# Joined small-tile stretches, one bfloat16 run per pair of the down projection, and a new order of small transfers in SP's queue

## The chip, the cores and the metric

The kernel runs on one core of one Trainium2 chip. The metric is the device time of one execution in microseconds. Engines are named as in the profile: PE (TensorE), PEld (its weight loads), DVE (VectorE), ACT (ScalarE), POOL (GpSimd) and SP (SyncE, which here only issues transfers; "SPq" is its queue). All but one of the transfers are issued by SP, in the order in which its instructions stand.

## What is computed

One transformer block with adaptive layer normalisation, S = 2048 rows of D = 1024, 32 heads of width 32, F = 3584, all in bfloat16:

```
sa, ca, ga, sb, cb, gb = silu(c) @ w_mod          # six rows of 1024
h   = layernorm(x) * (1 + ca) + sa
q, k, v = h @ wqkv ; pq, pk = phi(q), phi(k)      # phi(t) = t+1 if t>0 else exp(t), + 1e-6
kv  = pk^T v ; z = sum_s pk                       # per head
o   = (pq kv) / (pq z + 1e-6)
x   = x + ga * (o @ wo)
h   = layernorm(x) * (1 + cb) + sb
x   = x + gb * ((gelu(h @ w_gate) * (h @ w_up)) @ w_down)
```

## The kernel before, in words

A small recording layer (`sch.op`, `sch.dma`) notes every operation with what it reads and writes, derives the semaphore waits, and emits one instruction stream per engine, in the order recorded. Between two marks (from the end of the first k products to the second unit of the feed-forward part) `reorder` sorts the streams of DVE, ACT and POOL by a table of costs and due times; PE and SP keep the written order everywhere. SP's transfers run on eight semaphore lanes in turn, so a transfer also waits until the one eight places ahead of it has landed.

The stages on PE, with their places in the profiled execution:

- **q and k** (to about 127 us): layer norm, `q_block` and `kv_mm` products.
- **M** (127 to 191 us): instead of v, the kernel forms M = pk^T x, group by group (`m_tile`, L895: 16 matmuls of 128 x 341 or 342 make one tile; 24 tiles; output in PSUM banks 0 to 3 in turn). ACT copies each tile to MB, SP transposes MB by a transfer (`m_t`, notes mT0 to mT7, into two MTB buffers), and `kv_prod` (L913, eight 128 x 128 matmuls) multiplies by the v weights. The dictionary `HOOK` hangs other work behind tile n: "kv3" is `kv_prod(3)`; "modp" is `mod_pass` (eight matmuls on 32-column tiles, a copy, a store, and the loads sbT and cbT of the second shift and scale); "z32" prepares the denominators' weights; "den0" and "den1" are `den` (32 matmuls on 32-column tiles, then 1/den on DVE, L1245 and L1246, and a store to memory, the notes rden0.st and rden1.st); "w1" is `w2_pair(1)` (eight matmuls on 64 x 64 tiles); "gbr" is `gb_rows` (eight on 32-column tiles); "ps" is `pq_scale`, "rb" is `rb_load`: four transfers of 256 KB each that read 1/den back, broadcast over partitions, into RB. `rb_load(2, ...)` and `rb_load(1)` wait for rden1.st.
- **wo** (191 to about 257 us): after the last tile PE does parts of `wo_mm` (L1283), `w2_pair(2)`, `kv_prod(6)`, `kv_prod(7)`, `w2_pair(3)`, and then the chunks c0 to c15 of the output projection, two PSUM banks each, 2(c mod 4) and the next. DVE multiplies PQ by RB (`pq_scale`, L1273: four pieces per half of 512 rows, noted pqs sg.h.g0), adds each chunk to x (x1, L1291), and applies scale and shift of the second layer norm (h2mod, L724, which needs cb1, L1767, made from cbT). ACT makes the normalised rows, SP transposes them by transfers (T2). The dictionary `SLOT` hangs work behind chunk c; slot 2 held the scaling of PQ 1 and the load x7 of rows 7 to 9, slot 4 held cb1 and the first feed-forward weights (`wt_dma(0)`, two transfers).
- **feed-forward** (241 to 598 us): 28 units, each of seven products P1 to P7 (a Strassen-like scheme with sums ss and tp in fp32r; unit 0 runs P1, P2, P5, P6 before the rest of wo). P5 and P6 of unit 0 read ssum0 and ssum1 (L1413).
- **down projection** (598 us to the end): eight pairs of row chunks. In each pair `d_pair` runs seven products of 14 matmuls each in the order 1, 5, 6, 2, 7, 3, 4: P1 and P2 are bfloat16, the others fp32r. Their left sides are sums S0 to S4 (`d_s`, L1648; two halves each, S4 copied by ACT) of the activations ya.0 and ya.1, loaded by `y_in`; ACT copies (`dpcp`, `descp`) and DVE adds (`dpadd`, L1695) combine the banks b0 to b0+3; `evac` (L1576, L1577) scales, adds x and stores; `x_in` loads x (xq).

The matmul stream of M and the head of the wo stage stand in the code as

```
        for n, (g, k) in enumerate(tiles):
            m_tile(g, k, n % 4, n % 2)
            if n == len(tiles) - 1:
                kv_prod(5, 4)
            if k == 2:
                m_t(g)
            ...
            for f in HOOK.get(n, "").split():
                hook_run(f)
```

Of the kernel before, what the change touches and what calls it, by code (L numbers as in the profile page):

```python
# [8 lines left out]
ALU = mybir.AluOpType  # L9
# [321 lines left out]
def bass_adaLN_cond__linear_attn_block__geglu_ffn__prompt_kernel(  # L331
# [18 lines left out]
    with ExitStack() as es:  # L350
# [554 lines left out]
        def m_t(g):  # L905
            i = g % 2
            tdma(Q, MTB[i][:, :, :], MB[g][:, :], r_mb(g), r_mtb(i), f"mT{g}")

        def kv_prod(g, bank):
            i = g % 2  # L910
            o = None
            for dc in range(NDC):
                o = sch.op(T, lambda e, dc=dc: e.matmul(PS(bank, 0, P), WV[:, g, dc, :], MTB[i][:, dc, :],  # L913
                                                        start=(dc == 0), stop=(dc == NDC - 1)),
                           rd=r_wv(g) + r_mtb(i), pwr=(pr(bank) if dc == 0 else ()), note=f"kv g{g} dc{dc}")
            pset_writer(bank, o)
            z = 64 * (g % 2)
            for h in range(2):
                a, gz = 64 * h, g // 2 * 2 + h
                sch.op(V, lambda e, a=a, gz=gz: e.tensor_tensor(KVT[z:z + 64, gz, 0:64], ps_all[a:a + 64, bank * 512 + a:bank * 512 + a + 64], BMASK[a:a + 64, a:a + 64], ALU.mult),  # L920
                       prd=pr(bank), rd=r_sm("bmask"), wr=r_kvt(gz, gz + 1), note=f"kvt{g}", overwrite_ok=True)
# [270 lines left out]
        def z32():  # L1192
            sch.op(V, lambda e: e.tensor_tensor(Z32[:], BM32[:], ZCOLS[:, :].unsqueeze(2).to_broadcast([P, NG, NH]), ALU.mult),
                   rd=r_sm("bm32") + r_sm("zcols"), wr=r_sm("z32"), note="z32")

        def w2_pair(i, b0=4):
            for hf in range(2):
                for r in range(2):
                    for h in range(2):
                        b, g = b0 + 2 * r + hf, 2 * i + h  # L1200
                        sch.op(T, lambda e, b=b, g=g, h=h, r=r, hf=hf: e.matmul(ps_all[64 * h:64 * h + 64, b * 512:(b + 1) * 512], KVT[64 * r:64 * r + 64, g, 0:64],  # L1201
                               WO[64 * r:64 * r + 64, g, hf * 512:(hf + 1) * 512], start=True, stop=True),
                               rd=r_kvt(g, g + 1) + r_wo(g, hf * 512, (hf + 1) * 512), pwr=pr(b), note=f"w2 {i}.{hf}", overwrite_ok=True)
            for r in range(2):
                b, g = b0 + 2 * r, 2 * i + r
                w_, p_ = W2[:, g, :], ps_all[:, b * 512:(b + 2) * 512]
                eng = V if i > 1 and r else A
                sch.op(eng, lambda e, w_=w_, p_=p_, eng=eng: e.activation(w_, p_, ACTF.Copy) if eng == A else e.tensor_copy(w_, p_),
                       prd=pr(b) + pr(b + 1), wr=r_w(OFF_WK, "w2", g), note=f"w2cp{g}")
# [15 lines left out]
        def mod_pass():  # L1225
            assert mdone[0] >= 48 and not late
            mod_rows(((2, 4, 5, hl_src),))
            o_r = mod_store(4, 5, MROW[1], r_2k(OFF_ROW + 2048, "mrow1"), 1)
            for dst, nt, a0 in ((SBT, "sbT", 0), (CBT, "cbT", 2)):
                sch.dma(Q, lambda e, dst=dst, a0=a0: e.dma_start(dst[:, :], scr_row[1, a0:a0 + 2, :].rearrange("a (b p) -> p (a b)", p=P)),  # L1230
                        wr=r_sm(nt), deps=[o_r], note=nt)

# [33 lines left out]
        GH = [((0, 2), (2, 4)), ((4, 6), (6, 8))]  # L1266

        def pq_scale(sg, h, gs):
            i, t0 = sg % 2, h * HW
            for g0, g1 in gs:  # L1270
                ap = PQ[sg][:, g0:g1, t0:t0 + HW]
                rng = r_pq(sg, g0, g1, t0, t0 + HW)
                sch.op(V, lambda e, ap=ap, i=i, h=h, g0=g0, g1=g1: e.tensor_tensor(ap, ap, RB[i][:, h, g0:g1, :], ALU.mult),  # L1273
                       rd=rng + r_rb(i, h, g0, g1), wr=rng, deps=rb_ops[sg, h], note=f"pqs{sg}.{h}.{g0}")

        x1_ops, s_ops = {}, {}

        def wo_mm(c_, b0, gs):
# [9 lines left out]
            if gs[-1] == NG - 1:  # L1288
                for half in range(2):
# [3 lines left out]
                       prd=pr(b0) + pr(b0 + 1), rd=r_x(c_), wr=r_x(c_) + r_smc("st", c_, 48),  # L1293
                       deps=[s_ops[0, 0, 1]] if c_ == 13 else [], note=f"x1 c{c_}")
                if c_ < 2 * CPG:
# [5 lines left out]
        tiles = [(g, k) for g in range(4) for k in range(3)] + [(g, 0) for g in range(4, NG)] + [(g, k) for g in range(4, NG) for k in (1, 2)]  # L1301
        HOOK = {0: "ga", 6: "kv0", 10: "kv1", 11: "w0", 13: "kv2", 15: "modp kv3 z32", 16: "den0", 17: "w1 rb0.0 rb0.1", 18: "",
                19: "kv4", 20: "den1 ps0.0", 21: "gbr", 22: "ps0.1", 23: "rb2.0"}
        st = {}

        def hook_run(f):
# [11 lines left out]
            elif f[:3] == "den":  # L1318
                st[int(f[3:])] = den(int(f[3:]), 5)
                st[int(f[3:])]()  # L1320
# [7 lines left out]
        for n, (g, k) in enumerate(tiles):  # L1328
# [39 lines left out]
        def wt_dma(u):  # L1368
            i, f0 = u % 2, u % NFP * 256
            for t, v_ in enumerate((wg_v, wu_v)):  # L1370
                sch.dma(Q, lambda e, t=t, v_=v_: e.dma_start(WT[i][:, t, :, :], v_[:, :, f0:f0 + 256]), wr=r_wt(i, t, t + 1), note=f"wt{t} u{u}")

# [282 lines left out]
        def d_prod(ca, b0, k, own=None, js=None):  # L1655
            b = b0 + {1: 0, 2: 0, 5: 3, 6: 2, 7: 2, 4: 2, 3: 1}[k] if own is None else own
            i = {1: None, 2: None, 5: 0, 6: 1, 7: 2, 3: 3, 4: 4}[k]
            o = None
            js = range(nj(ca)) if js is None else js
            for j in js:  # L1660
# [5 lines left out]
                else:  # L1666
# [3 lines left out]
                    if i == 4:  # L1670
                        dst = dst.rearrange("p (h c) -> p h c", h=2)
                o = sch.op(T, lambda e, l_=l_, r_=r_, j=j, dst=dst: e.matmul(dst, l_[:, 0, :], r_, start=(k in (1, 5) or own is not None) and j == js[0], stop=j == js[-1], skip_group_check=True),  # L1672
                           rd=rl + rr, pwr=(pr(b) if j == js[0] else ()), note=f"down P{k} c{ca} j{j}", overwrite_ok=True)
# [30 lines left out]
        def d_pair0(hook):  # L1704
            parts = parts_of(0)
            for k in (2, 6, 5, 0, 7, 3, 13, 11, 12, 4):
# [13 lines left out]
                hook(k)  # L1720

        def d_pair(i, hook):
            ca, b0 = 2 * i, i % 2 * 4
# [6 lines left out]

            for k in (1, 5, 6, 2, 7, 3, 4):
                if last and k == 3:
                    d_prod(ca, b0, 3, None, range(6, NDJ))
                    evac_part(*parts[1])
                    continue
                d_prod(ca, b0, k)
                if k == 1:
                    d_cp(b0 + 2, b0, "dpcp")
                elif k == 5:
                    d_ecp(b0 + 3)  # L1740
                    d_s(ca, 2)
                elif k == 6:
                    d_add(b0 + 1, b0 + 2)
                    d_s(ca, 3)
                    y_next(0)
                elif k == 2:
                    evac(*parts[0])
                elif k == 7:
                    d_add(b0 + 3, b0 + 2)
                    d_s(ca, 4)  # L1750
                    y_next(1)
                    evac(*parts[3])
                elif k == 3:
# [12 lines left out]
        def cb1():  # L1766
            sch.op(V, lambda e: e.tensor_scalar(CB1T[:, :], CBT[:, :], 1.0, None, op0=ALU.add), rd=r_sm("cbT"), wr=r_sm("cb1T"))  # L1767
# [116 lines left out]
        def hooks(i):  # L1884
            def hook(k):
                more = i + 1 < 2 * CPG
                if i == 1:
                    if k == 1:
                        d_t(2, 5)
                        d_t(2, 6)  # L1890
                    if k in (6, 2, 7):
                        d_t(4, {6: 4, 2: 5, 7: 6}[k])
                    if k in (6, 7):
                        n = 1 if k == 6 else 2
                        evac(*parts_of(0)[n])
                        x_in(1, n)
                else:
                    if k == 1:
                        x_in(i, 0, 3, 1)
                    elif k == 5:  # L1900
                        x_in(i, 2)
                    if not more and k in (5, 6):
                        for q in {5: (0, 1), 6: (2,)}[k]:
                            t_gb(q)
            return hook

        d_pair0(hook0)
        for i in range(1, 2 * CPG):
            d_pair(i, hooks(i))
# [75 lines left out]
```

## Time and profile before

| what | value |
|---|---|
| time, median of 3 runs | 782.52 us (782.25 to 782.95) |
| span of the profiled execution (its own time between first and last instruction) | 780.9 us |
| median minus that span | 1.6 us |
| granted TensorE clock, mean | 1.000 |
| PE busy | 770.2 us (99%) |
| DVE busy | 645.9 us (83%) |
| ACT busy | 374.6 us (48%) |
| share of the chain that ended last on PE | 95% |

Starts are microseconds from the start of the span. A line of the timeline gives start, length (first start to last end of a merged group), engine, line of the kernel, operation, out<-in, and the number of instructions. A matmul line shows a pipelined length; the distance between starts is what a matmul costs. Some matmul records are missing, weight loads (PEld) are complete.

### The profile page before, as it was taken

How to read it: one execution, taken by the hardware profiler on the slowest of the kernel's cores; microseconds unless marked ns; L12 is line 12 of the kernel's file. 1: busy time of each engine (PE TensorE's matmuls, PEld its weight loads, DVE VectorE, ACT ScalarE, POOL GpSimd, SP SyncE). 2: the span in 40 equal slices, each digit the busy share in tenths (PEclk: the TensorE clock that was granted, in tenths of full speed). 3: DMA queues.
4: the chain of work that ended last, by engine and by line, in shares of the span. 5: the costliest groups of instructions: out<-in, count | busy, mean ns of one | idle time of the engine just before them, and what ended most of it. 6: DMA issues, size and time to landing. Idle time of an engine off the chain costs nothing.

```text
span 780.9 us, 10753 instructions
## 1 busy us (share of the span) xinstructions
PE 770.2 (99%) x3825; PEld 496.2 (64%) x3883; DVE 645.9 (83%) x964; ACT 374.6 (48%) x629; POOL 47.5 (6%) x126
## 2 busy tenths in 40 slices
PE   8999999999999999999999999999999999999998
PEld 4444445666445667667676767667676576677766
DVE  6699988897899878787989888888989888676767
ACT  2497743242466487878755555555555211111111
POOL 2031300000321011100000000000000000000000
PEclk9999999999999999999999999999999999999999
DMA  9879749939999358867353865535356334443331
GB/s 284 256 167 252 158 91 215 255 80 196 203 287 231 82 138 212 230 175 215 99 145 108 250 211 172 148 96 161 97 147 221 111 127 139 144 141 114 126 125 60
DMA packets 196940, 130.22 MB, mean 167 GB/s; under 512 B 69516, under 2 KB 182420, under 8 KB 195864
## 3 DMA queue, kind: packets, MB, share of 16 engines
q1 hardware_dynamic: 196872, 129.55, 62.4%
q8 instruction: 30, 0.49, 0.3%
q14 instruction: 22, 0.18, 0.1%
q10 hardware_dynamic: 16, 0.00, 0.0%
HBM read 92.55 MB, written 23.35 MB: 148 GB/s over the span
## 4 chain that ended last, share of the span: by engine, by line
PE 95%; SPq 2%; DMA 1%; DVE 1%; issue 1%; ACT 0%; DVEq 0%; ACTq 0%
PE ps_all L1458 45%; PE ps_all L1672 21%; PE ps_all L895 7%; PE ps_all L934 7%; PE ps_all L1283 7%; PE ps_all L880 5%; PE ps_all L1593 1%; SPq L598 1%; DMA wmq<-in_w_mod_dram 1%; SPq L603 1%; DMA h1T<-xh 0%; PE ps_all L913 0%; PE ps_all L1201 0%; PE ps_all L1240 0%; DVE h1T L724 0%
## 5 line engine op out<-in xcount | busy, mean ns | idle before, releaser
L1458 PE MATMUL ps_all<-ss,tp 128*128 128x512 f32 x896 | 214.3, 396 | 0.0
L1458 PEld LDWEIGHTS ps_all<-ss,tp 128*128 128x128 f32 x896 | 168.3, 188 | 37.8 <-DVE ss L1413 0.2
L1672 PE MATMUL ps_all<-dt,sb 128*128 128x512 f32 x424 | 102.5, 398 | 0.0
L1481 ACT ACTIVATE ge<-ps_all 128x512 f32<-128x512 f32 x112 | 64.1, 597 | 73.8 <-DVE ps_all L1469 62.1
L1458 PE MATMUL ps_all<-h2a,wt 128*128 128x512 bf16 x421 | 95.7, 379 | 1.8
L1672 PEld LDWEIGHTS ps_all<-dt,sb 128*128 128x128 f32 x424 | 79.6, 188 | 18.5 <-DVE sb L1648 0.3
L1476 DVE TENSOR_TENSOR ps_all<-ps_all,es 128x512 f32<-128x512 f32 x54 | 37.6, 699 | 49.4 <-ACT es L1466 49.0
L1488 DVE TENSOR_TENSOR ys<-ge,ps_all 128x512 bf16<-128x512 f32 x112 | 74.4, 684 | 3.8 <-PE ps_all L1672 0.5
L1458 PEld LDWEIGHTS ps_all<-h2a,wt 128*128 128x128 bf16 x448 | 38.0, 98 | 57.3 <-ACT ps_all L1463 16.9
L1433 DVE TENSOR_TENSOR tp<-wt 128x1024 fp32r<-128x1024 bf16 x56 | 68.1, 1217 | 1.8 <-DMA wt<-in_B_w_up_dram 1.8
L1433 DVE TENSOR_TENSOR tp<-wt,tp 128x1024 fp32r<-128x1024 bf16 x56 | 68.2, 1218 | 0.0
L934 PE MATMUL ps_all<-h1T,wq 128*128 128x512 bf16 x256 | 56.7, 379 | 0.0
L880 PE MATMUL ps_all<-wk,h1T 128*128 128x512 bf16 x239 | 55.3, 379 | 1.1 <-DMA wk<-in_A_wqkv_dram 0.5
L1283 PE MATMUL ps_all<-w,pq 128*128 128x512 bf16 x249 | 55.7, 379 | 0.5 <-issue 0.2
L1458 PE MATMUL ps_all<-ar,tp 128*128 128x512 f32 x224 | 55.5, 390 | 0.0
L869 ACT ACTIVATE eb<-ps_all 128x512 f32<-128x512 f32 x64 | 36.3, 594 | 37.6 <-PE ps_all L880 16.0
L1672 PE MATMUL ps_all<-wd,ya 128*128 128x512 bf16 x199 | 47.5, 380 | 0.7
L1458 PEld LDWEIGHTS ps_all<-ar,tp 128*128 128x128 f32 x224 | 42.1, 188 | 8.9
L1463 ACT ACTIVATE ps_all<-ps_all 128x512 f32<-128x512 f32 x56 | 32.6, 582 | 26.8 <-PE ps_all L1458 26.5
L934 PEld LDWEIGHTS ps_all<-h1T,wq 128*128 128x128 bf16 x256 | 25.0, 98 | 30.0
L1283 PEld LDWEIGHTS ps_all<-w,pq 128*128 128x128 bf16 x256 | 24.6, 98 | 30.3 <-issue 1.1
L1643 ACT ACTIVATE sb<-ya 128x896 fp32r<-128x896 bf16 (+1 forms) x16 | 14.5, 913 | 58.8 <-PE ps_all L1672 58.8
(141 smaller groups left out, 976.3 us busy)
## 6 DMA issues: line engine op xcount, KB each, us to landing
wt<-in_B_w_gate_dram SPq DMA_DIRECT2D x28, 512.0 KB, 4.0
wt<-in_B_w_up_dram SPq DMA_DIRECT2D x28, 512.0 KB, 5.2
scr_y<-ys SPq DMA_DIRECT2D x28, 512.0 KB, 3.2
ya<-scr_y SPq DMA_DIRECT2D x14, 896.0 KB, 4.9
rb<-scr_rd SPq DMA_DIRECT2D x32, 256.0 KB, 6.0
wd<-in_B_w_down_dram SPq DMA_DIRECT2D x7, 1024.0 KB, 7.6
wmst<-in_w_mod_dram SPq DMA_DIRECT2D x6, 1024.0 KB, 6.2
wmq<-in_w_mod_dram SPq DMA_DIRECT2D x8, 512.0 KB, 7.5
```

The costliest lines, as they stand in the source:

```text
L869: sch.op(A, lambda e: e.activation(EB[i][:, :], PS(bank), ACTF.Exp), prd=pr(bank), wr=rng, note=f"{note}.exp")
L880: o = sch.op(T, lambda e, dc=dc: e.matmul(PS(bank), H1[sg][:, ci, dc, :], W_[:, dc, jg * 512:(jg + 1) * 512], start=(dc == 0), stop=(dc == ...
L895: o = sch.op(T, lambda e, c_=c_: e.matmul(PS(bank, 0, n), PK[c_][:, g * P:(g + 1) * P], xrow(c_, o_, o_ + n), start=(c_ == 0), stop=(c_ == ...
L934: o = sch.op(T, lambda e, dc=dc: e.matmul(PS(b), WQ[:, dc, qc * P:(qc + 1) * P], H1[sg][:, :, dc, :], start=(dc == 0), stop=(dc == NDC - 1 ...
L1283: last[half] = sch.op(T, lambda e, g=g, half=half: e.matmul(PS(b0 + half), PQ[sg][:, g, ci * P:(ci + 1) * P], W2[:, g, half * 512:(half + ...
L1433: sch.op(V, lambda e: e.tensor_tensor(TP[k][:], in0, in1 if k in (0, 2) else in1[:], ALU.subtract), rd=r0 + r1, wr=r_tp(k), deps=[x1_ops[7 ...
L1458: o = sch.op(T, lambda e, l_=l_, r_=r_, dc=dc: e.matmul(PS(b), l_, r_, start=fresh and dc == 0, stop=dc == ND2 - 1, skip_group_check=True) ...
L1463: sch.op(A, lambda e: e.activation(PS(BB + t), PS(BA + t), ACTF.Copy), prd=pr(BA + t), pwr=pr(BB + t), note="pcp")
L1476: sch.op(V, lambda e: e.tensor_tensor(PS(BC + t), PS(BC + t), ES[t][:, :], ALU.add), prd=pr(BC + t), rd=r_2k(OFF_ES[t], f"es{t}"), pwr=pr( ...
L1481: sch.op(A, lambda e: e.activation(GE[i][:, :], PS(b), ACTF.Gelu_apprx_tanh), prd=pr(b), wr=r_2k(OFF_GE[i], f"ge{i}"), note="gelu")
L1488: sch.op(V, lambda e: e.tensor_tensor(YS[s_][:, 2 * h:2 * h + 2, t, :], q(GE[i][:, :]), q(PS(b + 1)), ALU.mult), rd=r_2k(OFF_GE[i], f"ge{i ...
L1672: o = sch.op(T, lambda e, l_=l_, r_=r_, j=j, dst=dst: e.matmul(dst, l_[:, 0, :], r_, start=(k in (1, 5) or own is not None) and j == js[0] ...
```

## The change

The diff does five things.

1. `HOOK`: modp moves from behind tile 15 to behind tile 16, ahead of den0, and w1 follows den0 at once; gbr moves from tile 21 to tile 20, behind den1. Banks change to fit: `mod_pass` uses 2 instead of 5, `gb_rows` 6 instead of 5, den0 3 instead of 5.
2. `rb_load(2, (0,))` moves from tile 23 to tile 22, and so stands ahead of mT7 in SP's queue; mrow2.st stands ahead of mT6.
3. The loads sbT and cbT leave `mod_pass`; `mod_load` issues them after the rb loads, behind x7 and `wt_dma(0)`, which move there from slots 2 and 4, all ahead of T2 0.
4. The scaling of PQ 1 is recorded before x1 c0, with dependences that hold DVE's order: pqs2.0.0, w2cp7, pqs2.0.2, pqs1.0 (four), x1 c0, c1, c2; pqs2.0.4 and pqs2.0.6 go behind x1 c4 and cb1.
5. Down projection, pairs 1 to 6: the order becomes 5, 6, 7, 2, P1 of the next pair, 3, 4. P7 gets bank b0+3 to itself, so `d_join` makes one more `descp` and one more `dpadd` per pair. Loads of xq 3 and 0 and the three d_t(4, q) sums of pair 1 change places.

```diff
-        HOOK = {..., 13: "kv2", 15: "modp kv3 z32", 16: "den0", 17: "w1 rb0.0 rb0.1", 18: "",
-                19: "kv4", 20: "den1 ps0.0", 21: "gbr", 22: "ps0.1", 23: "rb2.0"}
+        HOOK = {..., 13: "kv2", 15: "kv3 z32", 16: "modp den0 w1", 17: "rb0.0 rb0.1", 18: "",
+                19: "kv4", 20: "den1 gbr ps0.0", 22: "ps0.1 rb2.0"}
...
         rb_load(1)
         rb_load(2, (1,))
+        x_dma(NXR, 10)
+        wt_dma(0)
+        mod_load()
         w2_pair(3)
         wo_mm(1, 2, [3, 4, 5])
         wo_mm(2, 4, list(range(6)))
+        o_pq = pq_scale(1, 0, GH[0] + GH[1])
         for c_ in range(3):
             wo_mm(c_, 2 * c_, [6, 7])
...
-        pq_scale(2, 0, GH[0] + GH[1])
+        after.update({(2, 0, 0): kvt_op[:], (2, 0, 2): w2_op[:]})
+        pq_scale(2, 0, GH[0])
...
+        def d_join(b0):
+            d_ecp(b0 + 3)
+            d_add(b0 + 3, b0 + 1)
+            d_add(b0 + 2, b0 + 2)
+
+        def d_open(i):
+            b = i % 2 * 4
+            d_prod(2 * i, b, 1)
+            d_cp(b + 2, b, "dpcp")
...
-            for k in (1, 5, 6, 2, 7, 3, 4):
+            for k in ((5, 6, 2, 7, 3, 4) if last else (5, 6, 7, 2, 1, 3, 4)):
...
+                if k == 1:
+                    d_open(i + 1)
+                    hook(k)
+                    continue
                 d_prod(ca, b0, k)
...
-        SLOT = {2: lambda: (pq_scale(1, 0, GH[0] + GH[1]), x_dma(NXR, 10)),
+        SLOT = {2: lambda: None,
                 3: lambda: pq_scale(1, 1, GH[0] + GH[1]),
-                4: lambda: (cb1(), wt_dma(0)),
+                4: lambda: (cb1(), after.update({(2, 0, 4): [x1_ops[4]], (2, 0, 6): [x1_ops[4]]}), pq_scale(2, 0, GH[1])),
```

SP's queue around the moved transfers, each name one transfer (rb ones are groups of four):

```
before: ... mT5, rden1.st, mT6, mrow2.st, mT7, rb2.0, rb1.0, rb1.1, rb2.1, T2 0, x7, T2 1, T2 2, wt0, wt1, T2 3, ...
after:  ... mT5, rden1.st, mrow2.st, mT6, rb2.0, mT7, rb1.0, rb1.1, rb2.1, x7, wt0, wt1, sbT, cbT, T2 0, T2 1, T2 2, T2 3, ...
```

More of the change, by code (lines that the diff above doesn't have):

```diff
@@ L907, in m_t @@
             tdma(Q, MTB[i][:, :, :], MB[g][:, :], r_mb(g), r_mtb(i), f"mT{g}")
+        kvt_op = [None]
         def kv_prod(g, bank):
@@ L919, in kv_prod @@
                 a, gz = 64 * h, g // 2 * 2 + h
-                sch.op(V, lambda e, a=a, gz=gz: e.tensor_tensor(KVT[z:z + 64, gz, 0:64], ps_all[a:a + 64, bank * 512 + a:bank * 512 + a + 64], BMASK[a:a + 64, a:a + 64], ALU.mult),
+                kvt_op[0] = sch.op(V, lambda e, a=a, gz=gz: e.tensor_tensor(KVT[z:z + 64, gz, 0:64], ps_all[a:a + 64, bank * 512 + a:bank * 512 + a + 64], BMASK[a:a + 64, a:a + 64], ALU.mult),
                        prd=pr(bank), rd=r_sm("bmask"), wr=r_kvt(gz, gz + 1), note=f"kvt{g}", overwrite_ok=True)
@@ L1194, in z32 @@
                    rd=r_sm("bm32") + r_sm("zcols"), wr=r_sm("z32"), note="z32")
+        w2_op = [None]
         def w2_pair(i, b0=4):
@@ L1266, in bass_adaLN_cond__linear_attn_block__geglu_ffn__prompt_kernel @@
         GH = [((0, 2), (2, 4)), ((4, 6), (6, 8))]
+        after = {}
         def pq_scale(sg, h, gs):
-            i, t0 = sg % 2, h * HW
+            i, t0, ops = sg % 2, h * HW, []
             for g0, g1 in gs:
@@ L1272, in pq_scale @@
                 rng = r_pq(sg, g0, g1, t0, t0 + HW)
-                sch.op(V, lambda e, ap=ap, i=i, h=h, g0=g0, g1=g1: e.tensor_tensor(ap, ap, RB[i][:, h, g0:g1, :], ALU.mult),
-                       rd=rng + r_rb(i, h, g0, g1), wr=rng, deps=rb_ops[sg, h], note=f"pqs{sg}.{h}.{g0}")
+                o = sch.op(V, lambda e, ap=ap, i=i, h=h, g0=g0, g1=g1: e.tensor_tensor(ap, ap, RB[i][:, h, g0:g1, :], ALU.mult),
+                           rd=rng + r_rb(i, h, g0, g1), wr=rng, deps=rb_ops[sg, h] + after.get((sg, h, g0), []), note=f"pqs{sg}.{h}.{g0}")
+                ops.append(o)
+            return ops
         x1_ops, s_ops = {}, {}
@@ L1301, in bass_adaLN_cond__linear_attn_block__geglu_ffn__prompt_kernel @@
         tiles = [(g, k) for g in range(4) for k in range(3)] + [(g, 0) for g in range(4, NG)] + [(g, k) for g in range(4, NG) for k in (1, 2)]
-        HOOK = {0: "ga", 6: "kv0", 10: "kv1", 11: "w0", 13: "kv2", 15: "modp kv3 z32", 16: "den0", 17: "w1 rb0.0 rb0.1", 18: "",
-                19: "kv4", 20: "den1 ps0.0", 21: "gbr", 22: "ps0.1", 23: "rb2.0"}
+        HOOK = {0: "ga", 6: "kv0", 10: "kv1", 11: "w0", 13: "kv2", 15: "kv3 z32", 16: "modp den0 w1", 17: "rb0.0 rb0.1", 18: "",
+                19: "kv4", 20: "den1 gbr ps0.0", 22: "ps0.1 rb2.0"}
         st = {}
@@ L1349, in bass_adaLN_cond__linear_attn_block__geglu_ffn__prompt_kernel, with wt_dma @@
                 hook_run(f)
+        def wt_dma(u):
+            i, f0 = u % 2, u % NFP * 256
+            for t, v_ in enumerate((wg_v, wu_v)):
+                sch.dma(Q, lambda e, t=t, v_=v_: e.dma_start(WT[i][:, t, :, :], v_[:, :, f0:f0 + 256]), wr=r_wt(i, t, t + 1), note=f"wt{t} u{u}")
         wo_mm(0, 0, [0, 1, 2, 3])
@@ L1655, in d_prod @@
         def d_prod(ca, b0, k, own=None, js=None):
-            b = b0 + {1: 0, 2: 0, 5: 3, 6: 2, 7: 2, 4: 2, 3: 1}[k] if own is None else own
+            b = b0 + {1: 0, 2: 0, 5: 3, 6: 2, 7: 3 if 0 < ca < 4 * CPG - 2 else 2, 4: 2, 3: 1}[k] if own is None else own
             i = {1: None, 2: None, 5: 0, 6: 1, 7: 2, 3: 3, 4: 4}[k]
@@ L1671, in d_prod @@
                         dst = dst.rearrange("p (h c) -> p h c", h=2)
-                o = sch.op(T, lambda e, l_=l_, r_=r_, j=j, dst=dst: e.matmul(dst, l_[:, 0, :], r_, start=(k in (1, 5) or own is not None) and j == js[0], stop=j == js[-1], skip_group_check=True),
+                o = sch.op(T, lambda e, l_=l_, r_=r_, j=j, dst=dst: e.matmul(dst, l_[:, 0, :], r_, start=(k in (1, 5) or k == 7 and 0 < ca < 4 * CPG - 2 or own is not None) and j == js[0], stop=j == js[-1], skip_group_check=True),
                            rd=rl + rr, pwr=(pr(b) if j == js[0] else ()), note=f"down P{k} c{ca} j{j}", overwrite_ok=True)
@@ L1745, in d_pair @@
                     y_next(0)
+                elif k == 7:
+                    if last:
+                        d_add(b0 + 3, b0 + 2)
+                    else:
+                        d_join(b0)
+                    d_s(ca, 4)
+                    evac(*parts[3])
                 elif k == 2:
+                    y_next(1)
                     evac(*parts[0])
[L1748 to L1752, printed above, removed]
                 elif k == 3:
@@ L1896, in hook @@
                         x_in(1, n)
-                else:
[L1898 to L1901, printed above, removed]
+                    if k in (6, 7, 2):
+                        d_t(4, {6: 4, 7: 5, 2: 6}[k])
+                else:
+                    if k == 5:
+                        x_in(i, 1, 2)
                     if not more and k in (5, 6):
@@ L1904, in hook @@
                             t_gb(q)
+                if more and k in (1, 4):
+                    x_in(i + 1, 3 if k == 1 else 0)
             return hook
         d_pair0(hook0)
+        d_open(1)
+        d_t(2, 5)
+        d_t(2, 6)
         for i in range(1, 2 * CPG):
```

33 lines of the change are left out of this document (12 added, 21 removed).

## The prediction, made before the changed kernel ran

> **What bounds it now.** The page first: span and chain.
>
> ```profile
> span 780.9 us, 10753 instructions
> PE 95%; SPq 2%; DMA 1%; DVE 1%; issue 1%; ACT 0%; DVEq 0%; ACTq 0%
> ```
>
> Then the waits of PE, in total:
>
> ```profile
> PE ps_all L628 <- POOL bmask L581: 2.2, 1, 2.2
> PE ps_all L766 <- DMA wmq<-in_w_mod_dram: 1.0, 2, 0.6
> PE ps_all L880 <- DMA wk<-in_A_wqkv_dram: 0.5, 1, 0.5
> ```
>
> All of these lie in the first 28 us, which the change leaves alone. From there to the last product PE never waits, so any new wait of PE is added whole. A gain can come only from PE's own stream. Next, PE's timeline in M and the weight loads of one pair:
>
> ```profile
> 168.09 1.18 PE L895 MATMUL ps_all<-xrow,pk 128*128 128x342 bf16 x7
> 170.51 1.06 PE L1240 MATMUL ps_all<-pq,z 128*32 128x256 bf16 x32
> 171.50 1.19 PE L895 MATMUL ps_all<-xrow,pk 128*128 128x342 bf16 x7
> ...
> 176.81 1.18 PE L895 MATMUL ps_all<-xrow,pk 128*128 128x342 bf16 x7
> 179.15 0.61 PE L913 MATMUL ps_all<-mtb,wv 128*128 128x128 bf16 x8
> ...
> 194.57 1.05 PE L913 MATMUL ps_all<-mtb,wv 128*128 128x128 bf16 x16
> ```
>
> ```profile
> 645.54 2.71 PEld L1672 LDWEIGHTS ps_all<-wd,ya 128*128 128x128 bf16 x14 [0.26 <-issue]
> 654.98 2.70 PEld L1672 LDWEIGHTS ps_all<-wd,ya 128*128 128x128 bf16 x14 [0.26 <-issue]
> 667.58 2.71 PEld L1672 LDWEIGHTS ps_all<-wd,ya 128*128 128x128 bf16 x14 [0.26 <-issue]
> ```
>
> A tile of 16 takes 2.42 us (168.09 to 170.51) where 32-column work follows and 2.34 (176.81 to 179.15) where it does not. The line to remember is 194.57: kv_prod(6) and (7) run there, the second eight from 195.0. Last, SP's timeline, and the time to landing of four single transfers (the rden1.st store; mT5 issued at 180.55; mT7; the first rb2.0):
>
> ```profile
> 172.20 0.37 SPq L1230 DMA_DIRECT2D sbT<-scr_row  x1
> ...
> 185.74 0.35 SPq L1248 DMA_DIRECT2D scr_rd<-rdc  x1
> ...
> 191.15 1.26 SPq L703 DMA_TRANSPOSE mtb<-mb  x1
> 192.51 12.38 SPq L1260 DMA_DIRECT2D rb<-scr_rd  x16
> ```
>
> ```profile
> scr_rd<-rdc SPq DMA_DIRECT2D x1, 128.0 KB, 5.3
> mtb<-mb SPq DMA_TRANSPOSE x1, 9.0
> mtb<-mb SPq DMA_TRANSPOSE x1, 3.1
> rb<-scr_rd SPq DMA_DIRECT2D x1, 256.0 KB, 3.6
> ```
>
> The 9.0 is mT5 behind eight rb transfers; alone, mT7 takes 3.1. So a transfer waits for those ahead of it in SP's queue.
>
> **Gain in M.** Five stretches on small tiles (modr, den0, w1, den1, gbr) become two. A stretch costs 0.09 us going in (2.42 less 2.34) and about 0.1 coming out (den0's last group of matmuls takes 205 ns against 100 to 111 for those before). Two joins, modr with den0 and den1 with gbr, keep the tile size (128*32) and save 0.2 each. The third, den0 with w1, goes from 128*32 to 64*64, and no row shows that boundary: between 0 and 0.2. I take half: 0.5 in all. The Trainium skill (TensorEngine Tiling (Array Packing), Key Properties) says that a change of tiling mode drains the array; no run here shows it between two small modes, and by it the third join saves nothing and the sum is 0.1 later.
>
> **Gain in the down projection.** A pair lasts 22.04 us (645.54 to 667.58). Its 28 bfloat16 and 70 fp32r matmuls, at 216 and 227 ns from start to start, need 6.04 + 15.87 = 21.91. The rest, 0.13, is the price of two bfloat16 runs, 0.065 each. Six joins save 0.4.
>
> What covers this: count from T, the start of P4. P5 now follows P4 at once, 3.18 after T, and needs the first half of S0. DVE does evac part 1 first (x2b ends 1.70 after T at 666.10 in the trace), then 1.09 for the half: 2.8, so 0.4 to spare. P7 starts 9.8 after T; S2 follows S1 and evac part 2 and ends near 9.1. ya.0 must land before P1 of the next pair, 16.0 after T: it is issued behind out and xq near 9.5 and took 4.5 to 6.05 us: 14.0 to 15.5. ya.1 goes out behind out part 3, near 17.3, takes 4.7, lands at 22.0, and S0 wants it at 23.6. The added descp (0.60) and dpadd (0.70) lie beside P2 and P1. Only at the first junction (pair 1 to 2), where DVE also has three sums of 1.2 and one late evac, I count its queue 0.2 past P5's start (0 to 0.7). If a cover fails, up to 1 us per pair, 6 in all.
>
> **Cost 1: kv_prod(7) waits for mT7.** rb2.0 moves ahead of mT7 and waits for rden1.st to land. That store is issued at 185.74 behind rb0 and mT5 and lands at 191.1 (5.3 later; packets of a 16 KB instruction load lie among it, so 189.7 is possible). den1 comes only 0.4 earlier, and the queue ahead of it does not move. So SP stands at rb2.0 until 189.7 to 191.1, spends 4 x 0.46 on issues, and only then issues mT7, at 191.6 to 193.0 instead of 191.15. Ahead of its data now lie four rb of 256 KB. In the trace the fourth rb landed 7.2 after the first was issued (3.6 + 3 x 1.2); I allow 0.4 less, since mT7 was ahead of them then. mT7 follows 0.9 later (the distance of two transposes' landings): it lands at 197.4 to 199.2. PE is at kv_prod(7) at 195.0 - 0.5 = 194.5. Wait: 2.9 to 4.7, middle 3.9. Queued behind it: w2_pair(3) and all of wo. Net of M: +3.4. By the fit in the Trainium skill (DMA: Bandwidth & Descriptors, Anatomy of one DMA; made on the gpsimd path), 2.0 us and 436 GB/s, four rb would take 2.4 us instead of 4.8 and the wait would be near 1.5; the 1.2 us per rb in the trace decides.
>
> **Cost 2: cb1 waits for cbT.** cb1 is a DVE instruction between x1 c4 and the rest:
>
> ```profile
> 213.09 0.17 DVE L1767 TENSOR_SCALAR cb1T<-cbT 128x8 f32<-128x8 f32 x1
> 214.03 1.23 DVE L1291 SCALAR_TENSOR_TENSOR xall<-ps_all,xall 128x1024 bf16<-128x1024 f32 x1 [0.78 <-PE ps_all L1283]
> ...
> 224.04 1.23 DVE L1433 TENSOR_TENSOR tp<-wt 128x1024 fp32r<-128x1024 bf16 x1 [1.80 <-DMA wt<-in_B_w_up_dram]
> ...
> 243.67 2.35 DVE L1413 TENSOR_TENSOR ss<-ss,h2a 128x1024 fp32r<-128x1024 f32 x2
> ```
>
> Before, cbT went out at 172.62 and was long there. Now it stands behind 16 rb, x7, wt0 and wt1. The last rb landed at 215.1, its data ended near 212.4; the block starts 1.5 to 2.8 earlier and holds mT7 (0.9). Then x7 takes 2.0, wt0 and wt1 1.7 to 2.3 and 1.8, and the 4-byte packets of sbT and cbT ran from 173.2 to 175.3, 2.1. cbT lands at 218.5 to 222, I take 220. Behind it on DVE: pqs2.0.4 and .6 (1.2), then everything from x1 c5 to ssum1, 214.03 to 246.02 in the trace less the 1.8 and 0.3 it stood idle, 29.9. ssum1 is done at 220 + 0.2 + 1.2 + 29.9 = 251.3; P6 of unit 0, which reads it, started at 246.95. T2 0, now behind the same transfers, lands about 1 after cbT, and its first reader comes 6 after cb1: covered. So P6 starts 4.4 later than before (2.8 to 6.3).
>
> **The sum.** Both costs delay the same stream, so the larger counts, not both: cost 1 has brought PE to +3.4 when P6 finds DVE at +4.4. Then -0.4 and +0.2 for the down part: +4.2. Span 780.9 + 4.2 = 785.1; with the 1.6 us between span and median, 786.7. Moving x7 and wt0 earlier gains nothing: tsum's 1.8 us of DVE idle is not PE's.
>
> **Rivals.** 0.2% is 1.6 us, about what a measurement of this kernel can tell from no change.
> (a) Only cost 2 holds (mT7 not held up): P6 still at +4.4, the same time less what DVE gains by an earlier rb block: 785.5 to 787. For it: cost 2 does not need PE to be late. Against: the 9.0 of mT5.
> (b) The other side: rden1.st lands early, so that rb2.0 goes out while SP would only wait for ACT's copy for mT7 (190.62). For mT7 to land by 194.5 the fourth rb must land by 193.6 and the first go out by 186.4; that is the point from which it decides. The rb block then starts 6.1 earlier and cbT lands near 216, ssum1 is done at 247.3, 0.4 after P6's old start; with the down part's -0.2 the time is 782.7, and 781.8 if that last wait hides too. For it: the store itself is 128 KB and the 5.3 us are all queue. Against: rb0 and mT5 keep that queue full until 188.6.
> (c) The pairs lose a cover as well (S0 or ya.0), 0.5 to 1 us in six pairs: +3 to +6 on top, 790 to 793. For it: 0.4 us to spare at P5. Against: both half sums are counted from measured rows.
> (d) The joins save nothing: +0.9 on any case, 787.6 on the forecast.
>
> **Numbers.** Forecast with (a): 0.74, 784.9 to 788.8 on its own bounds; (b) 0.12; (c) 0.09; (d) 0.05. Time 786.7. The range 784.6 to 789.0 leaves out (b) and most of (c). Slower by over 0.2%: the forecast, (a), (c), (d), less their short ends: 0.86. Within: 0.1, from (b). Faster: 0.04.
>
> **What would show it.** Right: among PE's waits a new L913 on mtb of 3 to 5 us near 195, and an L1458 wait on DVE ss near 250 of about 1; DVE idle before L1767 by cbT of some us; bfloat16 runs of 28 weight loads, and a pair of 21.98. Wrong: mT7 landed by 195; no wait of PE after 28 us; or a wait of L1672 on sb or ya in every pair.

## The result, and the profile after

| | before | after |
|---|---|---|
| time, median of 5 runs | 782.50 us (782.13 to 782.95) | 788.72 us (787.61 to 789.14) |
| span of the profiled execution | 780.9 us | 785.8 us |
| ratio of the times | | 1.0074, 95% interval 1.0062 to 1.0086 |

The change costs 6.2 us. The execution of the changed kernel that was profiled is the fastest of its five (787.61); the spans of the other four are 786.2 to 787.3, and their mean granted TensorE clock is 0.996 to 0.998 instead of 1.000. The line numbers below are those of the changed kernel: L915 is `kv_prod` (L913 before), L1295 wo (L1283), L1303 x1 (L1291), L1799 cb1 (L1767), L1429 ss (L1413), L1474 the feed-forward products (L1458), L1689 the down products (L1672).

The span and the chain first. In the chain DMA, DVE and SP's queue now hold 11% where they held 4%:

```profile
span 785.8 us, 10828 instructions
PE 88%; DMA 5%; DVE 4%; SPq 2%; issue 1%; ACT 0%; POOL 0%; DVEq 0%; POOLq 0%; ACTq 0%
```

The waits of PE after the start (total, times, longest). Before, nothing stood here:

```profile
PE ps_all L915 <- DMA mtb<-mb: 3.7, 1, 3.7
...
PE ps_all L1474 <- DVE xall L1303: 0.8, 2, 0.5
...
PE ps_all L1474 <- DVE ss L1429: 0.3, 1, 0.3
```

SP's timeline (start, time of the issues). mT7 is the transpose at 191.94: it stands behind the four rb2.0 at 190.11, which went out when rden1.st had landed, at 190.09. The trace has mT7 landed at 197.81 and cbT at 220.30:

```profile
184.92 0.35 SPq L1256 DMA_DIRECT2D scr_rd<-rdc  x1
...
190.11 1.71 SPq L1268 DMA_DIRECT2D rb<-scr_rd  x4
191.94 1.23 SPq L703 DMA_TRANSPOSE mtb<-mb  x1
...
211.19 4.80 SPq L1238 DMA_DIRECT2D sbT<-scr_row  x1
216.03 1.71 SPq L1238 DMA_DIRECT2D cbT<-scr_row  x1
```

DVE's timeline at the same place: 5.55 us idle in front of cb1, and ssum1 (the second of the pair at 248.72) done at 251.07. It ended at 246.02 before:

```profile
220.33 0.17 DVE L1799 TENSOR_SCALAR cb1T<-cbT 128x8 f32<-128x8 f32 x1 [5.55 <-DMA cbT<-scr_row]
...
248.72 2.35 DVE L1429 TENSOR_TENSOR ss<-ss,h2a 128x1024 fp32r<-128x1024 f32 x2
```

Last the bfloat16 weight loads of the pairs. From 685.30 to 707.27 is 21.97 us, the period of an undisturbed pair. The run at 663.05 is cut by a wait for ya.0:

```profile
663.05 2.70 PEld L1689 LDWEIGHTS ps_all<-wd,ya 128*128 128x128 bf16 x14 [0.26 <-issue]
666.36 2.71 PEld L1689 LDWEIGHTS ps_all<-wd,ya 128*128 128x128 bf16 x14 [0.60 <-DMA ya<-scr_y]
685.30 5.72 PEld L1689 LDWEIGHTS ps_all<-wd,ya 128*128 128x128 bf16 x28 [0.26 <-issue]
```

The difference of the two profiled executions, by starts of the same PE instructions: -0.49 already ahead of M (start-up), -0.55 in M up to `kv_prod(6)`, +3.89 at `kv_prod(7)`, +1.29 from there to P5 of unit 0, +0.83 in the rest of unit 0, -0.06 in the other units, -0.06 in the down projection: +4.85 for a span that is 4.9 longer.

### The profile page after: what moved, and what is told of

It reads as the page before. It is cut to its first block, busy times and chain, and to the rows that moved or that the text cites. A ratio compares the mean times of both kernels' runs of the same rounds, so it can differ in the third digit from the quotient of the medians.

```text
span 785.8 us, 10828 instructions
## 1 busy us (share of the span) xinstructions
PE 774.4 (99%) x3883; PEld 497.1 (63%) x3883; DVE 647.6 (82%) x970; ACT 376.7 (48%) x635; POOL 47.5 (6%) x126
## 4 chain that ended last, share of the span: by engine, by line
PE 88%; DMA 5%; DVE 4%; SPq 2%; issue 1%; ACT 0%; POOL 0%; DVEq 0%; POOLq 0%; ACTq 0%
PE ps_all L1474 44%; PE ps_all L1689 20%; PE ps_all L936 7%; PE ps_all L880 7%; PE ps_all L895 6%; DMA rb<-scr_rd 3%; PE ps_all L1609 1%; DVE ss L1429 1%; SPq L1238 1%; DMA ya<-scr_y 1%; PE ps_all L951 1%; DMA scr_rd<-rdc 1%; DVE pq L1283 1%; DMA h2a<-xl 1%; SPq L1365 0%
## 5 line engine op out<-in xcount | busy, mean ns | idle before, releaser
L1474 PE MATMUL ps_all<-ss,tp 128*128 128x512 f32 x896 | 214.6, 396 | 1.0 <-DVE xall L1303 0.5
L1474 PEld LDWEIGHTS ps_all<-ss,tp 128*128 128x128 f32 x896 | 168.1, 188 | 39.8 <-DVE ss L1429 1.4
L1474 PE MATMUL ps_all<-h2a,wt 128*128 128x512 bf16 x448 | 101.5, 380 | 0.2 <-DVE xall L1303 0.2
L1689 PE MATMUL ps_all<-dt,sb 128*128 128x512 f32 x424 | 101.2, 394 | 0.0
L1689 PEld LDWEIGHTS ps_all<-dt,sb 128*128 128x128 f32 x424 | 79.5, 188 | 17.9 <-DVE sb L1665 0.5
L1474 PEld LDWEIGHTS ps_all<-h2a,wt 128*128 128x128 bf16 x448 | 37.9, 97 | 57.7 <-ACT ps_all L1479 16.9
L1295 PE MATMUL ps_all<-w,pq 128*128 128x512 bf16 x256 | 56.3, 379 | 0.0
L1474 PE MATMUL ps_all<-ar,tp 128*128 128x512 f32 x224 | 55.5, 390 | 0.0
L1715 ACT ACTIVATE de<-ps_all 128x512 f32<-128x512 f32 x14 | 8.4, 597 | 90.3 <-PE ps_all L1689 90.3
L1689 PE MATMUL ps_all<-wd,ya 128*128 128x512 bf16 x212 | 47.7, 380 | 0.1
L1474 PEld LDWEIGHTS ps_all<-ar,tp 128*128 128x128 f32 x224 | 42.0, 188 | 8.9
L1295 PEld LDWEIGHTS ps_all<-w,pq 128*128 128x128 bf16 x256 | 24.6, 98 | 30.2 <-issue 1.1
```

The lines of the kernel that those rows point to most:

```text
L1295: last[half] = sch.op(T, lambda e, g=g, half=half: e.matmul(PS(b0 + half), PQ[sg][:, g, ci * P:(ci + 1) * P], W2[:, g, half * 512:(half + ...
L1474: o = sch.op(T, lambda e, l_=l_, r_=r_, dc=dc: e.matmul(PS(b), l_, r_, start=fresh and dc == 0, stop=dc == ND2 - 1, skip_group_check=True) ...
```

## The experiments

Each kernel was timed beside the kernel before on the same chip: the first four rows stand against 782.49 us, the next four against 782.80, the last four against 782.67, so a difference between two groups carries up to 0.3 us of their own. All keep the joins in M and the new pair order. "Loads back" means that rb2.0 stands behind mT7 again, or that sbT and cbT are loaded at the end of `mod_pass`.

| kernel | what stays of the change besides joins and pair order | median, us | ratio to before |
|---|---|---|---|
| r_rb20 | late cbT, x7 and wt0 ahead, PQ by hand | 787.99 | 1.0072 (1.0058 to 1.0085) |
| r_cbt | rb2.0 ahead, x7 and wt0 ahead, PQ by hand | 788.33 | 1.0072 (1.0059 to 1.0084) |
| r_both | x7 and wt0 ahead, PQ by hand | 784.22 | 1.0019 (1.0010 to 1.0027) |
| cbt_ahead | all, with cbT ahead of x7 and wt0 | 786.64 | 1.0055 (1.0042 to 1.0067) |
| r_both_pq | x7 and wt0 ahead | 784.80 | 1.0022 (1.0013 to 1.0031) |
| rb_half | x7 and wt0 ahead, half of rb2.0 ahead | 785.15 | 1.0031 (1.0022 to 1.0041) |
| cbt_ahead_fill | as cbt_ahead, PE kept busy | 786.20 | 1.0043 (1.0031 to 1.0056) |
| joins_down | nothing | 782.18 | 0.9993 (0.9984 to 1.0002) |
| only_rb20 | rb2.0 ahead | 787.82 | 1.0064 (1.0050 to 1.0077) |
| only_late_cbt | late cbT, x7 and wt0 ahead | 787.01 | 1.0055 (1.0042 to 1.0067) |
| only_pq | PQ by hand | 784.53 | 1.0024 (1.0014 to 1.0034) |
| best | nothing, two xq loads moved | 781.80 | 0.9996 (0.9987 to 1.0004) |

**Either late load alone.** First each of the two costs was undone by itself.

```diff
-  20: "den1 gbr ps0.0", 22: "ps0.1 rb2.0"}
+  20: "den1 gbr ps0.0", 22: "ps0.1", 23: "rb2.0"}      # r_rb20
```

> The changed kernel with one edit: the first loads of rb2.0 go back behind mT7 in SP's queue. Theory (two late loads, the larger one counts): PE's wait of 3.7 us at kv_prod(7) disappears, but cbT still lands near 220, cb1 still waits, and the ss waits of PE in unit 0 grow from 0.3 us to some 3 to 4 in all; the time stays within 1 us of the changed kernel, 787.7 to 788.7 us. Rival (the wait for mT7 alone makes the loss, the late cbT is mostly hidden): 3.9 us come back, 784.8 us.

Measured 787.99, 0.7 below the changed kernel: the larger count stands almost alone. The waits of PE show where the 3.9 us went:

```profile
PE ps_all L1474 <- DVE xall L1303: 2.2, 2, 1.7
...
PE ps_all L1295 <- DVE xall L1303: 1.6, 1, 1.6
...
PE ps_all L1295 <- DVE pq L1283: 0.6, 1, 0.6
PE ps_all L1474 <- DVE ss L1429: 0.4, 2, 0.3
```

The wait at L915 is gone, 4.8 us of waits for DVE stand in its place, and P6 of unit 0 starts at 251.19 where it started at 251.13. Not all of it is at the ss sums, as expected, but most at x1. The 1.6 at L1295 was the first sign that more than cbT is late: it comes again below, where the PQ products stand alone (only_pq). The 2.2 for x1 at L1474 come again with the late cbT alone (only_late_cbt). The rival falls.

```diff
-  o_sc[0] = mod_store(4, 2, MROW[1], ..., 1)
+  o_sc[0] = mod_store(4, 2, MROW[1], ..., 1); mod_load()
...
-  mod_load()                                            # r_cbt
```

> The changed kernel with one edit: sbT and cbT are loaded at the end of mod_pass again, ahead of everything that was moved. Theory (two late loads, the larger one counts): the wait at kv_prod(7) stays at 3.5 to 4 us, DVE no longer waits before cb1, PE's waits in unit 0 (about 2.1 us by the trace of the changed kernel, from +2.84 after kv_prod(7) to +4.97 in steady units) disappear: 786.6 us, 786.0 to 787.1. Rival (x7 and wt0, issued ahead of unit 0's rows, cost DVE as much): 788 to 789 us.

Measured 788.33: a miss, and by number on the rival's side, but not for its reason. In this stretch DVE waits for no transfer but 0.8 us for rb, PE's waits in unit 0 are gone as expected, and the wait at L915 is 3.6. What takes the gain is something that neither theory had, the TensorE clock (below): 1.59 us behind that wait. A further 0.5 us is a wait for ya.0 in a pair of the down projection.

Then both edits together.

> The changed kernel with both loads back (rb2.0 behind mT7, sbT and cbT at the end of mod_pass); x7, wt0 and the hand-placed PQ products stay as changed. Theory: no wait of PE is left after 28 us, the joins in M keep their 0.55 us and the down projection its 0.05: 781.9 us, 781.4 to 782.4, beside 782.5 of the kernel before. Rival (the other moved transfers or the PQ products have a price of their own): 783 us or more.

Measured 784.22, 1.7 above the kernel before: a miss for the theory. Neither late load is there, but DVE's timeline shows x1 c0 (206.23) standing behind the PQ product that was placed ahead of it by hand, which waits for rb1.0:

```profile
203.70 2.50 DVE L1283 TENSOR_TENSOR pq<-pq,rb 128x512 bf16<-128x512 bf16 x4 [3.63 <-DMA rb<-scr_rd]
206.23 1.23 DVE L1303 SCALAR_TENSOR_TENSOR xall<-ps_all,xall 128x1024 bf16<-128x1024 f32 x1
```

PE waits 1.5 us for it at L1295. In the changed kernel the same product waits only 1.13 us for rb, and x1 c0 is waited for by nobody, since PE itself is 3.9 late: a third cost, hidden by the first.

**Where cbT stands.**

```diff
+  mod_load()
   x_dma(NXR, 10)
   wt_dma(0)
-  mod_load()                                            # cbt_ahead
```

> The changed kernel with sbT and cbT ahead of x7 and wt0 in SP's queue, still behind the rb loads. Theory (cbT is late because of what is queued ahead of it): it lands 3 to 5 us earlier, 215.5 to 217, DVE waits 1 to 2.5 us before cb1 instead of 5.6, and PE keeps the wait at kv_prod(7) and 0 to 0.8 us in unit 0: 786.6 to 787.4 us. Rival (it is late because of the 4-byte packets themselves, which hold SP for 4.8 us wherever they stand): x7, wt0 and T2 come as much later, and the time stays near 788.7 us.

Measured 786.64, 2.1 us below the changed kernel. cbT lands at 214.05, earlier than expected, and DVE does not wait for it at all. PE keeps one wait, 4.0 us at L915. So it was the place in the queue that made cbT late. SP's hold did not go with the 4-byte loads: it moved to x7, whose issue now takes from 207.24 to 212.61.

**The clock behind the wait.** The profile of this kernel, cut into stretches (PE busy, and further on PEclk, the granted clock): from 198.70 to 202.10 the clock is half.

```profile
core 0: us, PE busy (x) PEld busy (x) DVE busy (x) ACT busy (x) POOL busy (x), PEclk, DMA share, GB/s
194.00:197.50 3.50, 0.00 (x0) 0.00 (x0) 0.23 (x1) 0.00 (x0) 0.00 (x0) 1.00 1.22 234
198.70:202.10 3.40, 3.40 (x16) 0.84 (x15) 2.42 (x4) 1.02 (x1) 0.00 (x0) 0.52 0.93 193
```

From the last matmul of `kv_prod(7)` to the 19th matmul behind it, it takes 4.46 us; in the profile of the changed kernel, with the clock at 1.00, it takes 2.88. To test that the idleness is the cause, the wait was filled with work of no use:

```diff
   kv_prod(6, 4)
+  for _ in range(17):
+      sch.op(T, lambda e: e.matmul(PS(5), W2[:, 0, 0:P], W2[:, 0, 0:512], start=True, stop=True, ...), ...)
   kv_prod(7, 5)                                         # cbt_ahead_fill
```

> The kernel with sbT and cbT ahead of x7 and wt0, with 17 matmuls of no use (128x512, into the bank that kv_prod(7) opens afterwards) between kv_prod(6) and kv_prod(7), 3.7 us of work where PE waited 4.0. Theory (the wait lets the granted TensorE clock fall to half for about 3 us, which costs 1.5 us more): the clock stays at 1.0 and the time falls from 786.6 to 785.1 us, 784.8 to 785.5. Rival (the clock falls for another reason, the wait itself is all the loss): 786.6 us or more.

The same stretch of this kernel:

```profile
198.70:202.10 3.40, 3.40 (x22) 1.33 (x21) 3.02 (x5) 1.02 (x1) 0.00 (x0) 1.00 0.93 193
```

The clock stays full and the distance is 2.88 us again; the profiled span is 783.6, 1.2 below. That shows the idleness as the cause of the half clock. What it costs in time is shown less well: the median, 786.20, fell by 0.44 only (by 0.75 when each is taken against its own kernel before), and lies between the range expected and the rival's. Two of its five executions have 2.7 us between span and time where 1.8 to 2.0 is common, and the median of the spans falls by 0.7 (784.8 to 784.1), not by the 1.6 that the stretch regains. What the rest is stays open.

Why the profiled execution of the changed kernel kept its clock, though PE waited 3.7 us in it, can be read as well. Counted from the first rise to full speed, the granted clock changes in every profile that records it only after whole multiples of 3.413 us (in cbt_ahead at 7.71, 198.86 and 202.27: 0, 56 and 57 of them). Below are stretches of that length, cut on this grid: the first two lines are cbt_ahead, the last two the changed kernel.

```profile
195.44:198.86 3.42, 1.12 (x12) 0.76 (x12) 0.36 (x2) 0.00 (x0) 0.00 (x0) 1.00 1.21 229
198.86:202.27 3.41, 3.41 (x15) 0.93 (x14) 2.45 (x4) 1.02 (x1) 0.00 (x0) 0.50 0.96 199
192.56:195.97 3.41, 1.57 (x14) 0.76 (x11) 1.48 (x3) 0.82 (x1) 0.00 (x0) 1.00 0.97 197
195.97:199.39 3.42, 1.53 (x16) 0.88 (x20) 0.63 (x3) 0.00 (x0) 0.00 (x0) 1.00 1.28 256
```

In cbt_ahead PE was idle for 2.3 us of one stretch (2.5 in r_cbt, 2.6 in only_rb20), and the next ran at half clock. In the changed kernel the wait lay across the boundary, 1.8 us in one stretch and 1.9 in the next, and the clock stayed. So where the wait falls on the grid decides; the limit lies between 1.9 and 2.3 us of idleness in one stretch, and no run shows it closer.

**The price by dose.** All moves but x7 and wt0 undone (r_both_pq), and on that kernel rb2.0 split (rb_half):

```diff
-  o_pq = pq_scale(1, 0, GH[0] + GH[1])
+  o_pq = []
...
-  2: lambda: None,
+  2: lambda: pq_scale(1, 0, GH[0] + GH[1]),             # and (2, 0) whole in its old place; r_both_pq
```

```diff
-  20: "den1 gbr ps0.0", 22: "ps0.1 rb2.0"}
+  20: "den1 gbr ps0.0", 22: "ps0.1 rb2.0a", 23: "rb2.0b"}   # a: k = 0, 1; b: k = 2, 3; rb_half
```

> The changed kernel with rb2.0 behind mT7, sbT and cbT at the end of mod_pass, and the PQ products (1,0) and (2,0) in their old places; x7 and wt0 stay ahead. Theory formed from the last runs (the PQ product (1,0) ahead of x1 c0 makes PE wait for rb1.0, 1.7 us at wo, and leaves DVE 0.5 us late at the ss sums of unit 0): both waits go, 781.9 us, 781.5 to 782.4. Rival (x7 and wt0 in front of unit 0's rows make them late): 784 us as with both loads back.

> As the kernel with both loads and the PQ products back, but two of the four loads of rb2.0 go ahead of mT7 and two behind. Theory (mT7 waits for the data ahead of it, 1.2 us per load of 256 KB): PE waits 1.2 to 1.7 us at kv_prod(7), the TensorE clock stays at full speed, 783.3 us, 782.8 to 783.8. Rival (mT7 waits for the landing of rden1.st, whatever the loads behind it move): a wait of 3.5 to 4 us followed by a stretch at half clock, 787 us.

rb_half waits 1.7 us at L915, the upper end of what two loads at 1.2 us each foretell, against 3.6 to 4.6 with four ahead: the length of the wait is the data ahead of mT7, on top of the store's landing, and the rival falls. Its time, 785.15, is a miss, because its base is one too: r_both_pq has 784.80 and not 781.9. The rival named x7 and wt0, and its trace confirms it. DVE waits for the first transposed rows, T2 0:

```profile
221.32 2.14 DVE L724 TENSOR_SCALAR h2a<-h2a,cb1T,sbT 128x256 bf16<-128x256 bf16 x8 [3.74 <-DMA h2a<-xl]
```

T2 0 lands at 220.34 there and at 215.38 in joins_down, where x7 and wt0 stand behind it: 5 us for two weight loads and one of x. By the starts of the same weight loads PE falls back by 2.4 us against joins_down over unit 0, at waits for x1 and ss.

**One part at a time.** Last, each move alone, on a kernel that has only the joins and the pair order (joins_down: the kernel before with the new banks and hooks of M and with the new `d_pair`).

```diff
+  22: "ps0.1 rb2.0"                                     # only_rb20: this on joins_down
+  x_dma(NXR, 10); wt_dma(0); mod_load()                 # only_late_cbt: these behind rb_load(2, (1,))
+  o_pq = pq_scale(1, 0, GH[0] + GH[1])                  # only_pq: this and the hand-placed (2, 0)
```

> The kernel before with two parts of the change alone: the joined stretches in M and the one bfloat16 run per pair in the down projection. Theory: 0.55 us from M, 0.05 to 0.35 us from the pairs, no new wait but a few tenths at the junction of pairs 1 and 2: 781.7 us, 781.5 to 782.0. Rival (the joins gain nothing that a time shows): 782.5 us.

Measured 782.18, 0.6 below the kernel before and 0.2 above the range expected; the interval (0.9984 to 1.0002) just includes no change.

> The kernel with the joins in M and the new pair order (782.2 us), and rb2.0 moved ahead of mT7 as the only other move. Theory (each moved load is a loss by itself, and the losses cover one another): PE waits 3.6 to 4.2 us at kv_prod(7), in most executions a stretch at half clock of 1.5 us follows, nothing else: 787.4 us, 786.2 to 788.2. Rival (this wait is absorbed further on, since DVE gets ahead meanwhile): 784 to 786 us.

> The kernel with the joins in M and the new pair order, and of the other moves only x7, wt0, sbT and cbT behind the rb loads (rb2.0 behind mT7, the PQ products in their old places). Theory: no wait at kv_prod(7), cbT lands near 220, DVE waits 4 to 6 us before cb1, and PE waits some 5 to 5.5 us for x1 and ss up to unit 0's third product: 787.6 us, 786.8 to 788.3. Rival (without the wait at kv_prod(7) DVE has the x1 work of that time behind it and catches up): 784 to 786 us.

> The kernel with the joins in M and the new pair order, and of the other moves only the PQ products placed by hand. Theory: PE waits 1.5 to 1.9 us at wo, where x1 c0 stands behind the PQ product (1,0), which waits for rb1.0: 783.9 us, 783.5 to 784.3. Rival (both 0.5 us waits at the ss sums came from this order and not from x7 and wt0): 784.3 to 784.8 us.

The first two lie in the range expected, the third 0.2 above it and in the rival's: 787.82, 787.01 and 784.53, that is 5.6, 4.8 and 2.4 us above joins_down. In only_rb20 the wait is 4.6 us, the mean clock of all five executions 0.996 to 0.998, and nothing is absorbed later: the rival falls. In only_late_cbt the wait in front of cb1 is 8.1 us, longer than expected: DVE arrives 2 us earlier than in the changed kernel, and cbT lands at 220.86. PE's waits for pq, x1 and ss are 3.9 us in all, and by the end of unit 0 it has fallen back by 5.0 us against joins_down: a wait sets it back by more than its length (0.55 us in front of P5 by 0.9). In only_pq PE waits 1.9 us at L1295, and one ss wait of 0.3 remains, so the rival was half right. The parts sum to 12.8 us; together they cost 6.5 (788.72 less 782.18).

**A later place for xq.** The joins and the pair order, with two loads of x moved behind ya.0:

```diff
-  if k == 5:
+  if k == 6:
       x_in(i, 1, 2)                                     # best
```

> The kernel with the joins in M and the new pair order, and xq part 1 and 2 issued behind ya.0 instead of ahead of it in each pair. Theory: ya.0 goes out 0.85 us earlier, PE's wait of 0.2 to 0.35 us in the run of bfloat16 matmuls goes, every pair lasts 21.97 us: 0.2 us below the kernel without that edit, 0.9 below the kernel before, 781.7 to 782.2 us beside 782.8. Rival (ya.0 is slow because of the transfers beside it, not because of its place): no difference.

Measured 781.80, as expected, 0.9 below the median of the kernel before; the ratio of the means, 0.9996 (0.9987 to 1.0004), does not show it faster, and joins_down without this edit has 0.9993. The profile has no wait for ya.0, and from 657.50 on its runs are 21.97 us apart:

```profile
657.50 5.73 PEld L1672 LDWEIGHTS ps_all<-wd,ya 128*128 128x128 bf16 x28 [0.26 <-issue]
679.47 5.73 PEld L1672 LDWEIGHTS ps_all<-wd,ya 128*128 128x128 bf16 x28 [0.26 <-issue]
```

That is not yet the work of the edit. The profiles of r_both and only_late_cbt, which do not have it, show no wait of PE for ya.0 either, and in most pairs ya.0 goes out 3.50 us ahead of the run instead of 3.36 in joins_down: 0.14 us earlier and not 0.85. What this edit is worth is not shown.

## Why the prediction was right, point by point

**Gain in M.** Foreseen 0.5, measured 0.55. The two joins of equal tiles give 0.22 (den1 with gbr) and some 0.2. The third was put at half: den0's last group of matmuls still takes 202 ns in front of the 64 x 64 tiles, as it took 205 in front of a full tile, so the way out is paid and only the way in, 0.09, is saved. The trace agrees with the drain that the Trainium skill (TensorEngine Tiling (Array Packing), Key Properties) states for a change of tiling mode, here between two small modes; "it saves nothing" was too little by that 0.09.

**Cost 1.** rden1.st landed at 190.09 (189.7 to 191.1 foreseen), mT7 was issued at 191.94 (191.6 to 193.0) and landed at 197.81 (197.4 to 199.2); PE was held 3.89 us (middle 3.9). The row of 1.2 us per rb decided rightly: rb_half shows the dose, and the 1.5 us by the fit in the Trainium skill (DMA: Bandwidth & Descriptors, Anatomy of one DMA) was too little by 2.4.

**Cost 2.** cbT landed at 220.30 (220), ssum1 was done at 251.07 (251.3), P6 started 4.38 us later than before (4.4). Two small errors cancel in the 4.4: ssum1 came 0.2 earlier than foreseen, and P6's old start, taken as 246.95, is 246.75 in the trace before.

**The larger of the two, not both.** Right: with cost 1 taken away P6 starts at 251.19 instead of 251.13 and the time falls by 0.7 (r_rb20). With cost 2 taken away the time falls by 0.4 (r_cbt) or 2.1 (cbt_ahead); r_cbt alone does not show the rule, since 1.6 us at half clock and a wait for ya.0 took up its gain. The rule holds further than the prediction went. The PQ products by hand, and T2 0 behind x7 and wt0, were costed at nothing. That is true in this kernel, where PE does not wait for x1 c0 nor DVE for T2 0, but alone the PQ products cost 2.4 and x7 and wt0 cost 2.6. Of the rivals, (a) did not come, since PE did wait for mT7, and r_rb20, which makes its condition, has 787.99 and not 785.5 to 787; (b) did not come, since the store landed at 190.09 and not before 186.4; 784.2 in r_both, with neither load late, suggests that its 782 was too low besides, though no run had its condition. (c) shows in one run of a pair, not in six, and (d) falls with the 0.55 of M. Its +0.9 was too much in any case: 0.5 of it is M's, which by the rule of the larger is not in the sum.

**What was mis-sized.** Three terms.
First, I stopped at P6. The next product that reads an ss sum also waited for DVE, at 257.0 (0.3 us idle and a slow restart), and P5 ahead of P6 for x1; unit 0 ends 0.6 later than P6 alone would make it. That the sum came out 0.7 under the profiled difference (4.2 for 4.9) is this term and the next.
Second, the down projection: the pair came out as foreseen (21.97 for 21.98), but the 0.4 from six joins was eaten by 0.35 instead of 0.2. The wait was not P5's for its sums at the first junction (0.07 there) but P1's for ya.0, in the run that opens pair 3. ya.0 was issued 9.7 us after T and took 6.3 where I had allowed 6.05. The cover was counted and too thin; in other profiles the wait fell into this pair, another, several (rb_half) or none.
Third, the largest: the profiled span plus 1.6 gives 787.4, the median is 788.7. Of this 0.2 is the time between span and measured time, 1.8 to 1.9 us in this kernel; the rest goes with the clock. The four executions that were not profiled ran at a mean clock of 0.996 to 0.998, and their spans are 0.4 to 1.5 us longer than the profiled one. One stretch of 3.41 us at half clock makes a mean of 0.998 over 786 us and two make 0.996, so these executions had, by this estimate, one or two. Every execution of r_cbt, cbt_ahead and only_rb20, whose profiles have a wait of 3.6 us or more for mT7, shows 0.996 to 0.998 as well, while r_rb20 and only_late_cbt, which lose as much by shorter waits, show 0.999 or 1.000. The step that failed is "any new wait of PE is added whole": a wait of this length is mostly added with a slow stretch behind it. The Trainium skill (TensorE: Matmul & The Clock Gate, What's actually happening) says that the clock falls to half after an idle window of about 3.4 us and that the window runs freely. That speaks against this change, and it should have stood in the prediction beside the 3.9 us. The traces agree on the length, 3.41 us, and on the free running. They differ in that no window was idle throughout: 2.3 us of one were enough in cbt_ahead, while 1.9 us in the profiled execution of the changed kernel were not.

That the median lies within 784.6 to 789.0 is in part luck. The upper end comes from the late end of cost 2, no term of the sum stands for a slow clock, and the median is only 0.3 below that end; one of the five executions, 789.14, is above it.

## What to carry to other kernels

A load that is moved ahead in a queue is paid by every load that it passes; find for each of these the first reader and the time left, the transposes and the 4 KB rows included. Where several moves fall into one stretch, their costs cover one another: undoing one shows little, so price each alone on a kernel that has none of the others. A wait of PE of 3.5 us or more should be priced with a slow stretch behind it: 1.6 us here where it was one stretch of 3.41 us, 2.3 us in only_rb20 where it was two, and nothing in the one profile where the wait was split between two stretches.

## What the runs showed of the hardware

- After PE waits of 3.6 to 4.6 us the granted clock was 0.50 for 3.41 us in r_cbt and cbt_ahead, which cost 1.6 us, and for 6.83 us in only_rb20, which cost 2.3 (PE is 4.7 us later than in joins_down at `kv_prod(7)` and 7.0 behind the slow stretch). The change came on a grid of 3.413 us, behind a stretch with 2.3 to 2.6 us of idleness; 1.9 us in one stretch left the clock full. After waits up to 1.9 us in r_both, r_rb20 and only_pq the mean clock stayed at 0.999 to 1.000. In rb_half three of ten executions show 0.998, and their waits are not known. Seventeen matmuls of no use in place of the wait kept it at 1.00.
- SP's own issue of a transfer, else 0.3 to 0.6 us for a load, took 3.8 us at wt1 and 4.8 at sbT in the changed kernel and 5.4 at x7 in cbt_ahead. In both the first two transfers behind the sixteen rb loads went out in 0.4 us and the third was held, so its place decides and not its size: sbT, 4 KB, took 0.4 us as the first.
- Two times in the same program, the wait for ya.0 and the time between span and measured time (1.7 to 3.0 us), differ from execution to execution by more than the 0.2 us that the later place for xq was to bring; neither the time nor one trace shows such an edit.
